# Pooling the keys with a halving addition and accumulating products instead of a reduction

## The chip, the cores and the metric

One core of a Trainium2 chip runs the whole program. Its engines are TensorE (PE in the profile; its loads of the stationary operand are PEld), VectorE (DVE), ScalarE (ACT), GpSimd (POOL) and SyncE (SP), which issues most of the DMAs. Each engine works through its own instructions in the order in which they were written and waits on semaphores for the others. The metric is the device time of one execution in microseconds; lower is better.

## The reference

Three layers one after the other, all in float32:

```python
# attention, B, H, S, D = 4, 8, 576, 64; keys and values are pooled by 8
k_p = k.reshape(B, H, S // 8, 8, D).mean(axis=3)        # 72 pooled keys per head
v_p = v.reshape(B, H, S // 8, 8, D).mean(axis=3)
scores = np.matmul(q, k_p.transpose(0, 1, 3, 2)) / np.sqrt(D)
attn = softmax(scores);  x = np.matmul(attn, v_p)       # -> x: 2304 tokens x 512

# a mixture of 8 experts with balanced shares P (8 rounds of row and column scaling)
for e in range(8):
    out += P[:, e:e+1] * (np.maximum(x @ w1[e], 0) @ w2[e])

# one more layer: softplus(x @ w_in) @ w_out, 512 -> 2048 -> 512
```

The change touches only the pooling of the keys and values, that is `k_p` and `v_p`.

## The kernel before, in words

**Attention in steps.** The attention is cut into 32 steps, m = 0 to 31. A step takes one pair of heads and half of the 576 queries of one batch (288, in three tiles of 96). The first ten steps, m < AHEAD = 10, run at the front of the kernel with nothing else beside them but the preparation of the first expert weights (`sums_w1(0)` after step 4, `prep_w1(0)` after step 6). The other 22 are laid between the products of the experts, which keep TensorE busy for the rest of the run.

**One step** (`attn_step`, L391): TensorE turns the queries of the next step, channels first (`pq`, L288; ScalarE copies them to `qT`), and multiplies those of this step with the block-diagonal pooled keys `kbd` (`s`, L311). VectorE takes the maximum of each row (`mx`, L317) and subtracts it (`ex`, L318), ScalarE takes the exponential. One step later VectorE sums and inverts (`divide`, L325 to L327), GpSimd multiplies (L328). Another step later TensorE turns the result (`pa`, L339), ScalarE copies it to `aT`, and TensorE multiplies it with the pooled values `vp` (`px`, L349, `mix`); ScalarE copies `px` to the input of the experts.

**Pooling** (`pool_kv`, L265). A pair of heads of one batch has one tile of keys `kt` and one of values `vt`, each 72 partitions x 2 heads x 8 positions x 64 channels. There are 16 pairs, i = 0 to 15. The keys are summed over the 8 positions by one VectorE reduction (`kp`, L269). The values of the first four pairs are summed by three halving additions on GpSimd (L271 to L273), the others by a VectorE reduction (L275). `keys_first` (L293) then turns `kp` on TensorE into a bank `pk` with a transpose (L297), and VectorE scales the two halves of it into `kbd` (L299).

**Order.** Everything is written out by hand. `pool_at` says at the end of which step a pair is pooled, and `turn_at` in which step its keys are turned: one step later. Pairs 0 and 1 are pooled ahead of step 0, pair 2 in step 0, pair 3 in step 1, pairs 4 to 7 in steps 3, 5, 7 and 9, and pair 8 in step 11. Within a step the order is: turn the queries, scores and maximum, the gate of finished tokens, turn the older softmax, turn the keys that were pooled in the step before, exponential, divide, mix, and at the end pool the next pair. Loads of further keys and values are issued behind the pooling of a pair (L278).

After step 9 the tokens of the first group are split into differences and remainders (`ta`, L437; `xhi`, L467; `xlo`, L471), and the products of the experts begin (`p`, L530).

Of the kernel before, what the change touches and what calls it, by code (L numbers as in the profile page):

```python
# [9 lines left out]
F32 = mybir.dt.float32  # L10
# [3 lines left out]
ALU = mybir.AluOpType  # L14
AX = mybir.AxisListType
# [4 lines left out]
def attention_moe_softplus_kernel(  # L20
# [12 lines left out]
    nc = tc.nc  # L33
    B, H, S, D = q.shape
# [4 lines left out]
    POOL = 8  # L39
    SP = S // POOL  # L40
    HP = H // 2
# [37 lines left out]
    def bank(name, kind="y", dt=F32):  # L79
        kind = kind if kind in banks else ""  # L80
        return banks[kind].tile([P, 512], dt, tag=f"bank{kind}", name=name)
# [7 lines left out]
    ident = cpool.tile([P, P], F32, name="ident")  # L89
# [74 lines left out]
    def pool_add(o, a, b):  # L164
        nc.gpsimd.tensor_tensor(o, a, b, op=ALU.add)
# [53 lines left out]
    at_p = actx.enter_context(tc.tile_pool(name="at", bufs=2))  # L219
# [8 lines left out]
    AHEAD = 10  # L228
# [13 lines left out]
    def load_kv(pool):  # L242
        i = next_kv[0]
        if i >= B * HP:
            return
        next_kv[0] += 1
        b, h0 = i // HP, i % HP * 2
        kt = pool.tile([SP, 2, POOL, D], F32, tag="k", name="kt")
        vt = pool.tile([SP, 2, POOL, D], F32, tag="v", name="vt")
        nc.sync.dma_start(kt, k[b, h0:h0 + 2].rearrange("h (p t) d -> p h t d", t=POOL))  # L250
        nc.sync.dma_start(vt, v[b, h0:h0 + 2].rearrange("h (p t) d -> p h t d", t=POOL))
        kv_t[i] = kt, vt, pool
# [11 lines left out]

    def pool_kv(i):  # L265
        kt, vt, pool = kv_t.pop(i)
        kp = at_p.tile([SP, 2, D], F32, tag="kp", name="kp", bufs=1)
        vp = at_p.tile([SP, 2, D], F32, tag="vp", name="vp", bufs=NK + 1)
        nc.vector.tensor_reduce(kp, kt.rearrange("p h t d -> p h d t"), axis=AX.X, op=ALU.add)  # L269
        if i < HP:  # L270
            pool_add(vt[:, :, 0:4, :], vt[:, :, 0:4, :], vt[:, :, 4:8, :])  # L271
            pool_add(vt[:, :, 0:2, :], vt[:, :, 0:2, :], vt[:, :, 2:4, :])
            pool_add(vp, vt[:, :, 0, :], vt[:, :, 1, :])  # L273
        else:
            nc.vector.tensor_reduce(vp, vt.rearrange("p h t d -> p h d t"), axis=AX.X, op=ALU.add)  # L275
        pooled[i] = kp, vp

        if pool is ld_p or next_kv[0] < 2 * HP:  # L278
            load_kv(pool)

    def channels_first(m):

        qt = q_l.pop(m)
        pq = bank("pq")
        qT = at_p.tile([P, W], F32, tag="qT", name="qT")
        for j in range(JH):
            src = qt[:, j].rearrange("p h d -> p (h d)")
            nc.tensor.transpose(pq[:, j * QP:(j + 1) * QP], src, ident[:QP, :QP])  # L288
        nc.scalar.copy(qT, pq[:, :W])
        q_t[m] = qT  # L290
        load_q(m + NQ)

    def keys_first(i):  # L293

        kp = pooled[i][0]
        pk = bank("pk")
        nc.tensor.transpose(pk[:, :SP], kp.rearrange("p h d -> p (h d)"), ident[:SP, :SP])  # L297
        for h in range(2):
            nc.vector.tensor_scalar_mul(  # L299
                kbd[i % NK][h * D:(h + 1) * D, h * SP:(h + 1) * SP],  # L300
                pk[h * D:(h + 1) * D, :SP],
                1.0 / POOL / math.sqrt(D),
            )
# [29 lines left out]
    def turn_attn():  # L333
        m, ex = to_turn.pop(0)
        aT = at_p.tile([SP, 2, W], F32, tag="aT", name="aT")
        for h in range(2):
            pa = bank("pa")
            for j in range(JH):
                nc.tensor.transpose(pa[:SP, j * QP:(j + 1) * QP], ex[:, 2 * j + h, :], ident[:QP, :QP])  # L339
            nc.scalar.copy(aT[:, h, :], pa[:SP, :W])  # L340
        to_mix.append((m, aT))
# [38 lines left out]


    pool_at = {}
    for i in range(2, B * HP):
        b, hp = divmod(i, HP)
        pool_at.setdefault(hp - 2 if b == 0 else 2 * HP * b - 5 + 2 * hp, []).append(i)
    turn_at = {}
    for m, l in pool_at.items():
        turn_at.setdefault(m + 1, []).extend(l)
    turn_at.setdefault(0, []).append(1)

    def attn_step(m, early):  # L391


        last = STEPS
        if m + 1 < last:
            channels_first(m + 1)
        if m < last:
            exp, divide = softmax(m)
        while to_gate:
            gate()  # L400
        while to_turn:
            turn_attn()
        for i in turn_at.get(m, ()):
            keys_first(i)
        if m < last:
            exp()
            to_divide.append(divide)
        while len(to_divide) > (1 if early else 0):
            to_divide.pop(0)()
        while len(to_mix) > (0 if early or m >= last else 1):  # L410
            mix()
        for i in pool_at.get(m, ()):
            pool_kv(i)

    for i, pool in enumerate((ld_e, ld_e, ld_p, ld_p)):
        load_kv(pool)
# [6 lines left out]
    load_w(1, 0)  # L423
    load_w(2, 0)
    pool_kv(0)
    channels_first(0)
    keys_first(0)
    pool_kv(1)
    nc.gpsimd.memset(ones, 1.0)

# [602 lines left out]
```

## Time and profile before

| | |
|---|---|
| time, median of 3 runs | 2063.92 us (2063.12 to 2064.44) |
| profiled execution: its span, the one time that its page gives | 2065.1 us |
| TensorE busy | 2021.1 us, 98% of the span |
| VectorE busy | 1446.1 us, 70% |
| GpSimd busy | 1233.9 us, 60% |
| ScalarE busy | 837.6 us, 41% |

The profile records one execution. Its page gives the busy time of each engine and the chain of work that ended last, followed back from the end: at each step to what released it. A timeline lists the instructions by their start; the column after the start is how long they took, and the bracket at the end is the idle time of the engine just before, with what ended it. A stretch of time can be cut into windows, with busy time, granted clock of TensorE (1.00 is the full 2.4 GHz, 0.50 the lower level of 1.2 GHz) and the share of the DMA engines. A matrix product or a transpose can show up as several instructions, and matmul ends are modelled, since they are pipelined.

### The profile page before, as it was taken

What the parts mean: (1) busy time and instruction counts of PE and PEld (TensorE: products, weight loads), DVE (VectorE), ACT (ScalarE), POOL (GpSimd) and SP (SyncE); (2) the same over time, 40 slices, a digit from 0 to 9 for tenths busy, and PEclk for the clock granted to TensorE, in tenths of its full rate; (3) what the DMA queues carried; (4) which work ended last, traced back from release to release, by engine and by line L of the source; (5) the groups of instructions that cost most, each with busy time, mean ns of one, the idle gap of its engine ahead of it and who ended that gap; (6) DMA issues with size and microseconds to landing.
All of it is one profiled execution on the core that took longest, in us unless ns stands there. A gap on an engine that the chain in (4) does not pass through costs nothing.

```text
span 2065.1 us, 27617 instructions
## 1 busy us (share of the span) xinstructions
PE 2021.1 (98%) x10285; PEld 1746.1 (85%) x10285; DVE 1446.1 (70%) x2477; ACT 837.6 (41%) x1583; POOL 1233.9 (60%) x993
## 2 busy tenths in 40 slices
PE   7899999999999999999999999999999999999998
PEld 5677888888888888888888888888888888888887
DVE  7787587875666767777776776777777666767756
ACT  4555545454322433222243222222222356565554
POOL 4666689886556555556565555655555554544555
PEclk9799999999999999999999999999999999999999
DMA  6353233444223222232242222322222111121132
GB/s 183 89 141 108 86 94 103 142 150 144 67 92 126 76 92 86 82 92 78 91 154 72 87 82 77 92 73 86 92 82 82 62 53 50 62 87 52 62 118 72
DMA packets 133762, 192.00 MB, mean 93 GB/s; under 512 B 26924, under 2 KB 82940, under 8 KB 133628
## 3 DMA queue, kind: packets, MB, share of 16 engines
q1 hardware_dynamic: 129596, 183.82, 28.5%
q10 hardware_dynamic: 4032, 6.42, 0.8%
q8 instruction: 80, 1.31, 0.3%
q14 instruction: 54, 0.44, 0.1%
HBM read 166.94 MB, written 23.27 MB: 92 GB/s over the span
## 4 chain that ended last, share of the span: by engine, by line
PE 88%; DVE 6%; ACT 3%; POOL 2%; issue 1%; DMA 1%; SPq 0%; ACTq 0%; POOLq 0%; DVEq 0%
PE py L530 44%; PE p L530 32%; PE ph L530 9%; POOL w1lo L168 1%; DVE kp L269 1%; PE s L311 1%; ACT w1hi L199 1%; DVE vp L275 1%; PE px L349 1%; PE pa L339 0%; POOL w2lo L168 0%; PE pt L692 0%; ACT xhi L467 0%; DVE mx L317 0%; DVE s L325 0%
## 5 line engine op out<-in xcount | busy, mean ns | idle before, releaser
L530 PE MATMUL py<-w2hi,hhi 128*128 128x512 f32 x1440 | 567.9, 394 | 5.0 <-DVE g L686 2.7
L530 PE MATMUL py<-w2hi,hlo 128*128 128x512 f32 x1440 | 562.7, 391 | 0.8 <-POOL hlo L573 0.8
L530 PE MATMUL py<-w2lo,hhi 128*128 128x512 f32 x1440 | 562.5, 391 | 0.0
L168 POOL TENSOR_TENSOR w1lo<-w1raw,w1hi 128x512 fp32r<-128x512 f32 (+1 forms) x216 | 252.2, 1186 | 458.2 <-ACT w1hi L199 357.8
L530 PE MATMUL p<-xhi,w1hi 128*128 128x448 f32 (+1 forms) x1344 | 459.9, 342 | 9.8 <-DVE p L610 3.6
L530 PE MATMUL p<-xlo,w1hi 128*128 128x448 f32 (+1 forms) x1344 | 457.7, 341 | 3.4 <-DVE xlo L471 3.3
L530 PE MATMUL p<-xhi,w1lo 128*128 128x448 f32 (+1 forms) x1344 | 457.3, 340 | 3.7 <-POOL w1lo L168 3.7
L686 DVE SCALAR_TENSOR_TENSOR g<-py,prob,g 128x512 f32<-128x512 f32 x482 | 360.4, 748 | 99.2 <-PE py L530 87.8
L545 ACT ACTIVATE hhi<-p 128x448 fp32r<-128x448 f32 (+1 forms) x384 | 180.9, 495 | 414.1 <-PE p L530 380.1
L530 PEld LDWEIGHTS py<-w2hi,hhi 128*128 128x128 f32 x1440 | 271.2, 188 | 65.9 <-DVE g L686 4.6
L530 PEld LDWEIGHTS py<-w2hi,hlo 128*128 128x128 f32 x1440 | 271.0, 188 | 60.9 <-POOL hlo L573 1.7
L168 POOL TENSOR_TENSOR w2lo<-w2raw,w2hi 128x1024 fp32r<-128x1024 f32 x120 | 289.0, 2408 | 51.5 <-ACT w2hi L212 46.3
L530 PEld LDWEIGHTS py<-w2lo,hhi 128*128 128x128 f32 x1440 | 271.3, 188 | 49.9
L530 PEld LDWEIGHTS p<-xhi,w1hi 128*128 128x128 f32 x1344 | 256.5, 191 | 38.4 <-DVE p L610 4.7
L530 PEld LDWEIGHTS p<-xlo,w1hi 128*128 128x128 f32 x1344 | 256.6, 191 | 22.6 <-DVE xlo L471 3.9
L530 PEld LDWEIGHTS p<-xhi,w1lo 128*128 128x128 f32 x1344 | 256.9, 191 | 17.8 <-POOL w1lo L168 4.9
L612 ACT COPY za<-p 128x448 f32<-128x448 f32 (+1 forms) x96 | 46.0, 479 | 477.0 <-PE p L530 472.8
L546 DVE SCALAR_TENSOR_TENSOR hlo<-p,hhi 128x448 fp32r<-128x448 f32 (+1 forms) x384 | 210.3, 549 | 32.9 <-ACT hhi L545 32.4
L168 POOL TENSOR_TENSOR w1lo<-sums,w1hi 128x1024 fp32r<-128x1024 f32 x96 | 231.4, 2410 | 0.0
L610 DVE TENSOR_TENSOR za<-p,za 128x448 f32<-128x448 f32 (+1 forms) x96 | 53.4, 556 | 166.9 <-PE p L530 166.8
L780 POOL TENSOR_TENSOR dt<-dt,dr 128x512 f32<-128x512 f32 x32 | 41.5, 1295 | 150.5 <-DVE dr L779 150.5
L573 POOL TENSOR_TENSOR hlo<-ln,hhi 128x448 fp32r<-128x448 f32 (+1 forms) x80 | 97.3, 1218 | 51.8 <-ACT hhi L572 51.5
(123 smaller groups left out, 2707.6 us busy)
## 6 DMA issues: line engine op xcount, KB each, us to landing
w1raw<-in_moe_w_dram SPq DMA_DIRECT2D x96, 512.0 KB
w2raw<-in_moe_w_dram SPq DMA_DIRECT2D x96, 512.0 KB
w1raw<-v SPq DMA_DIRECT2D x24, 512.0 KB
w2raw<-v SPq DMA_DIRECT2D x24, 512.0 KB
f<-in_moe_w_in_dram SPq DMA_DIRECT2D x16, 512.0 KB
v<-dt SPq DMA_DIRECT2D x32, 256.0 KB
f<-in_moe_w_out_dram SPq DMA_DIRECT2D x16, 512.0 KB
xlod<-xl ACTq DMA_DIRECT2D x28, 224.0 KB
```

Source lines behind the costliest of these rows:

```text
L168: nc.gpsimd.tensor_tensor(o, a, b, op=ALU.subtract)
L199: nc.scalar.copy(at(hi), src)
L269: nc.vector.tensor_reduce(kp, kt.rearrange("p h t d -> p h d t"), axis=AX.X, op=ALU.add)
L275: nc.vector.tensor_reduce(vp, vt.rearrange("p h t d -> p h d t"), axis=AX.X, op=ALU.add)
L530: nc.tensor.matmul(ps, lhs[a], rhs[b], start=first and i == 0, stop=last and i == 2, skip_group_check=goes_on,)
L545: nc.scalar.activation(hh, src, AF.Relu)
L546: nc.vector.scalar_tensor_tensor(hl, src, 0.0, hh.bitcast(F32), op0=ALU.max, op1=ALU.subtract)
L573: nc.gpsimd.tensor_tensor(hl, l, hh.bitcast(F32), op=ALU.subtract)
L610: add = lambda o, x, y: nc.vector.tensor_tensor(o, x, y, op=ALU.add)
L612: nc.scalar.copy(a, pa)
L686: nc.vector.scalar_tensor_tensor(a, py, prob[:, t, e:e + 1], a, op0=ALU.mult, op1=ALU.add)
L780: nc.gpsimd.tensor_tensor(t, t, r.bitcast(F32), op=ALU.add)
```

## The change

For the pairs that are pooled in steps 0 to 9 and ahead of them (i = 0 to 7), the reduction and the transpose of the keys go. In their place VectorE adds the second four positions of `kt` onto the first four, in place, and TensorE multiplies what is left, position by position and head by head, with the identity, and accumulates: eight products of 72 x 64 with 72 x 72 that leave the pooled keys, already channels first, in `pk`. The scaling into `kbd` stays. The keys of such a pair are now turned in the step in which it is pooled and not in the next, and the pooling stands ahead of the exponential, the division and the mix, not at the step's end. The values of pairs 4 to 7 move from a VectorE reduction to the three GpSimd additions. Pairs 8 to 15 are pooled and turned as before.

```diff
--- before.py
+++ after.py
@@ -264,16 +264,21 @@
 
     def pool_kv(i):
         kt, vt, pool = kv_t.pop(i)
-        kp = at_p.tile([SP, 2, D], F32, tag="kp", name="kp", bufs=1)
         vp = at_p.tile([SP, 2, D], F32, tag="vp", name="vp", bufs=NK + 1)
-        nc.vector.tensor_reduce(kp, kt.rearrange("p h t d -> p h d t"), axis=AX.X, op=ALU.add)
-        if i < HP:
+        early = pooled_at[i] < AHEAD
+        kp = None
+        if not early:
+            kp = at_p.tile([SP, 2, D], F32, tag="kp", name="kp", bufs=1)
+            nc.vector.tensor_reduce(kp, kt.rearrange("p h t d -> p h d t"), axis=AX.X, op=ALU.add)
+        if early:
             pool_add(vt[:, :, 0:4, :], vt[:, :, 0:4, :], vt[:, :, 4:8, :])
             pool_add(vt[:, :, 0:2, :], vt[:, :, 0:2, :], vt[:, :, 2:4, :])
             pool_add(vp, vt[:, :, 0, :], vt[:, :, 1, :])
         else:
             nc.vector.tensor_reduce(vp, vt.rearrange("p h t d -> p h d t"), axis=AX.X, op=ALU.add)
         pooled[i] = kp, vp
+        if early:
+            keys_first(i, kt)
 
         if pool is ld_p or next_kv[0] < 2 * HP:
             load_kv(pool)
@@ -290,11 +295,21 @@
         q_t[m] = qT
         load_q(m + NQ)
 
-    def keys_first(i):
+    def keys_first(i, kt=None):
 
         kp = pooled[i][0]
         pk = bank("pk")
-        nc.tensor.transpose(pk[:, :SP], kp.rearrange("p h d -> p (h d)"), ident[:SP, :SP])
+        if kt is None:
+            nc.tensor.transpose(pk[:, :SP], kp.rearrange("p h d -> p (h d)"), ident[:SP, :SP])
+        else:
+            half = POOL // 2
+            nc.vector.tensor_tensor(kt[:, :, 0:half, :], kt[:, :, 0:half, :], kt[:, :, half:POOL, :], op=ALU.add)
+            for t in range(half):
+                for h in range(2):
+                    nc.tensor.matmul(
+                        pk[h * D:(h + 1) * D, :SP], kt[:, h, t, :], ident[:SP, :SP],
+                        start=t == 0, stop=t == half - 1,
+                    )
         for h in range(2):
             nc.vector.tensor_scalar_mul(
                 kbd[i % NK][h * D:(h + 1) * D, h * SP:(h + 1) * SP],
@@ -380,13 +395,15 @@
 
 
     pool_at = {}
+    pooled_at = {0: -1, 1: -1}
     for i in range(2, B * HP):
         b, hp = divmod(i, HP)
-        pool_at.setdefault(hp - 2 if b == 0 else 2 * HP * b - 5 + 2 * hp, []).append(i)
+        pooled_at[i] = hp - 2 if b == 0 else 2 * HP * b - 5 + 2 * hp
+        pool_at.setdefault(pooled_at[i], []).append(i)
     turn_at = {}
     for m, l in pool_at.items():
-        turn_at.setdefault(m + 1, []).extend(l)
-    turn_at.setdefault(0, []).append(1)
+        if m >= AHEAD:
+            turn_at.setdefault(m + 1, []).extend(l)
 
     def attn_step(m, early):
 
@@ -402,6 +419,9 @@
             turn_attn()
         for i in turn_at.get(m, ()):
             keys_first(i)
+        if m < AHEAD:
+            for i in pool_at.get(m, ()):
+                pool_kv(i)
         if m < last:
             exp()
             to_divide.append(divide)
@@ -409,8 +429,9 @@
             to_divide.pop(0)()
         while len(to_mix) > (0 if early or m >= last else 1):
             mix()
-        for i in pool_at.get(m, ()):
-            pool_kv(i)
+        if m >= AHEAD:
+            for i in pool_at.get(m, ()):
+                pool_kv(i)
 
     for i, pool in enumerate((ld_e, ld_e, ld_p, ld_p)):
         load_kv(pool)
@@ -424,7 +445,6 @@
     load_w(2, 0)
     pool_kv(0)
     channels_first(0)
-    keys_first(0)
     pool_kv(1)
     nc.gpsimd.memset(ones, 1.0)
```

The order of TensorE's instructions from the program's start to the scores of step 1, before (`pq` turned queries, `s` scores, `pk` pooled keys; the number at `kbd` is the buffer, one per pair of heads):

```order
L288 MATMUL pq<-ident,qt 128x96 x3
L297 MATMUL pk<-ident,kp 128x72
L288 MATMUL pq<-ident,qt 128x96 x3
L311 MATMUL s<-kbd_126,qT 96x144 x3
L297 MATMUL pk<-ident,kp 128x72
L288 MATMUL pq<-ident,qt 128x96 x3
L311 MATMUL s<-kbd_127,qT 96x144 x3
```

And the same stretch after the change:

```order
L309 MATMUL pk<-ident,kt 64x72 x8
L293 MATMUL pq<-ident,qt 128x96 x3
L309 MATMUL pk<-ident,kt 64x72 x8
L293 MATMUL pq<-ident,qt 128x96 x3
L326 MATMUL s<-kbd_126,qT 96x144 x3
L309 MATMUL pk<-ident,kt 64x72 x8
L293 MATMUL pq<-ident,qt 128x96 x3
L326 MATMUL s<-kbd_127,qT 96x144 x3
```

The keys of pair 1 now stand ahead of the scores of step 0, and those of pair 2 ahead of the scores of step 1; before, each stood behind them.

VectorE's instructions in step 3, to the maximum of step 4, before (`s` in the rows of L325 and L326 is the row sum; `vp` pooled values):

```order
L317 TENSOR_REDUCE mx<-s 96x6
L318 TENSOR_TENSOR ex<-s,mx 96x432
L325 TENSOR_REDUCE s<-ex 96x6
L326 TENSOR_SCALAR s<-s 96x6
L327 RECIPROCAL sm<-s 96x6
L269 TENSOR_REDUCE kp<-kt 72x128
L275 TENSOR_REDUCE vp<-vt 72x128
L317 TENSOR_REDUCE mx<-s 96x6
```

And after:

```order
L332 TENSOR_REDUCE mx<-s 96x6
L333 TENSOR_TENSOR ex<-s,mx 96x432
L306 TENSOR_TENSOR kt<-kt 72x2x256
L314 TENSOR_SCALAR kbd_130<-pk 64x72 x2
L340 TENSOR_REDUCE s<-ex 96x6
L341 TENSOR_SCALAR s<-s 96x6
L342 RECIPROCAL sm<-s 96x6
L332 TENSOR_REDUCE mx<-s 96x6
```

The two reductions behind the division are gone. Ahead of it stand the halving addition and the two scalings, which read what TensorE makes of that addition.

GpSimd's instructions from the preparation of the first weights (`w1lo`, after step 6) on, before (`ex` is the multiplication of L328):

```order
L168 TENSOR_TENSOR w1lo<-w1raw,w1hi 128x512
L168 TENSOR_TENSOR w1lo<-w1raw,w1hi 128x256
L168 TENSOR_TENSOR w1lo<-sums,w1hi 128x1024
L328 TENSOR_TENSOR ex<-ex,sm 96x432 x3
L437 TENSOR_TENSOR tb<-g_92 128x512
```

And after:

```order
L168 TENSOR_TENSOR w1lo<-w1raw,w1hi 128x512
L168 TENSOR_TENSOR w1lo<-w1raw,w1hi 128x256
L168 TENSOR_TENSOR w1lo<-sums,w1hi 128x1024
L165 TENSOR_TENSOR vt<-vt 72x2x256
L165 TENSOR_TENSOR vt<-vt 72x2x128
L165 TENSOR_TENSOR vp<-vt 72x128
L343 TENSOR_TENSOR ex<-ex,sm 96x432 x2
L165 TENSOR_TENSOR vt<-vt 72x2x256
L165 TENSOR_TENSOR vt<-vt 72x2x128
L165 TENSOR_TENSOR vp<-vt 72x128
L343 TENSOR_TENSOR ex<-ex,sm 96x432
```

The additions for the values of pair 6 stand between the weights and the multiplication of step 7, and those of pair 7 ahead of the multiplication of step 9.

## Rows read from the trace of the kernel before

**Rows 1.** Chain of waits, 0 to 110 us, its shares by line.

```profile
by line: PE p L530 16.3%; DVE kp L269 8.4%; PE py L530 7.7%; PE s L311 6.5%; POOL w1lo L168 5.4%; PE px L349 5.3%; DVE vp L275 4.9%; PE pa L339 4.5%; DMA kt<-in_k_dram 4.1%; issue 3.7%; DVE mx L317 3.6%; DVE s L325 3.0%; DVE ex L318 2.8%; P
```

**Rows 2.** Windows: length, busy PE, PEld, DVE, ACT, POOL, then clock, DMA share, GB/s.

```profile
20.00:28.00 8.00, 8.00 (x36) 6.27 (x35) 5.90 (x10) 3.27 (x8) 1.81 (x2) 1.00 0.87 233
28.00:40.00 12.00, 8.73 (x86) 5.60 (x84) 11.28 (x24) 7.25 (x22) 5.21 (x7) 1.00 0.46 112
42.00:50.00 8.00, 7.47 (x32) 5.15 (x30) 5.61 (x9) 3.47 (x10) 4.29 (x4) 0.50 0.65 178
```

**Rows 3.** Groups by shape, 0 to 60 us: busy us, mean ns | idle before.

```profile
L269 DVE TENSOR_REDUCE kp<-kt 72x128 f32<-72x1024 f32 x8 | 15.1, 1892 | 4.8 <-DMA kt<-in_k_dram 4.8
...
L275 DVE TENSOR_REDUCE vp<-vt 72x128 f32<-72x1024 f32 x4 | 7.6, 1900 | 0.0
...
L299 DVE TENSOR_SCALAR kbd<-pk 64x72 f32<-64x72 f32 x14 | 3.2, 226 | 1.5 <-PE pk L297 1.4
...
L471 DVE TENSOR_TENSOR xlo<-tb,xhi 128x512 fp32r<-128x512 f32 x1 | 1.3, 1346 | 0.3 <-ACT xhi L467 0.3
...
L471 DVE TENSOR_TENSOR xlo<-ta,xhi 128x512 fp32r<-128x512 f32 x1 | 0.7, 692 | 0.0
```

**Rows 4.** Timeline of the opening, steps 0 to 2: start us, length us.

```profile
8.16 1.90 DVE L269 TENSOR_REDUCE kp<-kt 72x128 f32<-72x1024 f32 x1 [0.39 <-DMA kt<-in_k_dram]
...
10.09 0.60 DVE L317 TENSOR_REDUCE mx<-s 96x6 f32<-96x432 f32 x1
...
13.10 2.06 POOL L165 TENSOR_TENSOR vt<-vt 72x512 f32<-72x512 f32 x2 [0.92 <-DMA vt<-in_v_dram]
...
13.68 0.60 DVE L317 TENSOR_REDUCE mx<-s 96x6 f32<-96x432 f32 x1
...
15.24 0.45 POOL L165 TENSOR_TENSOR vp<-vt 72x128 f32<-72x128 f32 x1
...
17.36 1.17 PE L339 MATMUL pa<-ident,ex 96*72 96x96 f32 x6 [0.18 <-POOL ex L328]
```

**Rows 5.** Timeline of step 3 and the start of step 4.

```profile
20.17 0.74 PE L288 MATMUL pq<-ident,qt 96*128 96x96 f32 x3
...
20.70 1.65 PE L311 MATMUL s<-kbd,qT 128*96 128x144 f32 x6
...
22.39 0.60 DVE L317 TENSOR_REDUCE mx<-s 96x6 f32<-96x432 f32 x1 [1.86 <-PE s L311]
...
23.31 1.70 PE L349 MATMUL px<-aT,vp 72*64 72x288 f32 x4
...
23.62 0.60 DVE L325 TENSOR_REDUCE s<-ex 96x6 f32<-96x432 f32 x1
...
24.57 1.88 DVE L269 TENSOR_REDUCE kp<-kt 72x128 f32<-72x1024 f32 x1
...
24.95 0.74 PE L288 MATMUL pq<-ident,qt 96*128 96x96 f32 x3
```

**Rows 6.** Timeline, steps 5 to 9 and the first products of the experts.

```profile
29.20 0.47 PE L288 MATMUL pq<-ident,qt 96*128 96x96 f32 x3
...
34.15 0.90 PE L311 MATMUL s<-kbd,qT 128*96 128x144 f32 x6
...
34.98 0.69 PE L371 MATMUL pg<-g,wg 128*8 128x72 f32 x32
...
38.01 0.47 PE L288 MATMUL pq<-ident,qt 96*128 96x96 f32 x3
...
42.14 2.38 POOL L168 TENSOR_TENSOR w1lo<-sums,w1hi 128x1024 fp32r<-128x1024 f32 x1
...
44.46 0.92 POOL L328 TENSOR_TENSOR ex<-ex,sm 96x432 f32<-96x432 f32 x1
...
48.25 0.74 PE L288 MATMUL pq<-ident,qt 96*128 96x96 f32 x3
...
57.57 0.58 PE L530 MATMUL p<-xlo,w1hi 128*128 128x256 f32 x1 [3.27 <-DVE xlo L471]
```

## The prediction

> **What bounds the kernel now.** I read the chain of waits first, for the stretch up to 110 us, since the change touches nothing but the first ten attention steps and the first products behind them. There the reader sees the reductions of the keys with 8.4% and those of the values with 4.9% of 110 us, 14.6 us together [rows 1]: VectorE's pooling is on the path that sets the end. Everything behind is the experts' products, which follow from whenever the front is done, so a microsecond gained or lost in the front is one in the total. Then the windows: from 28 to 40 us VectorE is busy for 11.28 of 12 us and TensorE for 8.73, so VectorE bounds there; from 20 to 28 us TensorE is busy for all 8 us and VectorE for 5.90, and from 42 to 50 us TensorE for 7.47 us and VectorE for 5.61 [rows 2]. So the bound changes hands, and TensorE's clock decides it: from 42 to 50 us the granted clock is 0.50, which is 1.2 GHz, and from 28 to 40 us it is 1.00, 2.4 GHz. For 20 to 28 us the column says 1.00, but the six score instructions take 1.65 us there and 0.90 us later [rows 5, 6], so I take the opening to run at the lower level. Last the timeline, step by step, from one start of a turn of queries to the next: steps 3 to 5 take 9.03 us (20.17 to 29.20), 5 to 7 take 8.81 and 7 to 9 take 10.24 [rows 5, 6].
>
> **What the change removes.** Eight reductions of keys of 1.89 us and four of values of 1.90 us [rows 3], 22.7 us of VectorE. It adds eight halving additions of 72 x 512; the row of the same shape and kind over 128 partitions, a remainder, is 0.69 us [rows 3], so 5.5 us. VectorE's two scalings (0.226 us each, 0.45 us together) stay.
>
> **What it adds on TensorE.** Eight products per pair instead of one transpose. The trace has no such group, so I bound it. From below: the gate's 32 instructions of the same moving width, 72, take 0.69 us at the full level [rows 6]; a program's float32 product shows as two instructions, so 16 instructions at that rate are 0.35 us, or 0.63 us at the lower level, by the ratio 1.65/0.90 of the scores. From above: six score instructions with twice the columns (144), one behind the other, take 1.65 us at the lower level [rows 5]; sixteen of half the width, none beside another, are 2.2 us. The gate writes to four groups of columns at once, the new products to two, so I take twice the gate's time: 0.69 us at the full level, 1.27 us at the lower. That is the nearest row; a gain below zero is excluded, as 16 instructions replace one.
>
> **What it moves, and what then waits.** This decides. Before, a reduction ran one step ahead, while TensorE did the scores, and its transpose stood behind them. Now VectorE's halving stands behind the subtraction of its own step, the products wait for it on TensorE, the two scalings wait for the products on VectorE, and behind them wait the division of the last step, GpSimd's multiplication and so TensorE's next turn. On TensorE the next step's queries and scores are queued behind the products, though they don't need those keys yet.
>
> Opening. The keys of pair 1 land at about 8.1 us, as VectorE's wait shows [rows 4]. Then: halving 0.69, products 1.27, queries and scores 2.18 (20.17 to 20.70 + 1.65) [rows 5]: the maximum of step 0 starts at 12.3 us, not at 10.09 [rows 4]. From one maximum to the next it was 3.59 us (10.09 to 13.68 [rows 4]), set by VectorE; now it is the loop maximum and subtraction 1.23 (22.39 to 23.62 [rows 5]), halving 0.69, products 1.27, queries and scores 2.18, 5.4 us. The maximum of step 1 is at 17.7 us; then 1.23 + 0.69 + 1.27, scalings 0.45, division 0.95 (23.62 to 24.57), multiplication 0.92 [rows 3, 5, 6] lead to the first turn of a softmax at 23.2 us, where it was at 17.36 [rows 4]. **+5.9 us.** Nothing absorbs it: VectorE's reductions wait 4.8 us in all for keys to land [rows 3], for the first two pairs alone.
>
> Steps 3 to 5, at the lower level: the products start after 2.18 + 1.23 + 0.69 = 4.1 us, end at 5.4, the mix and the way to the next step are 1.64 us (23.31 to 24.95 [rows 5]): 7.0. The even step is TensorE's 4.78 us (20.17 to 24.95). 11.8 against 9.03, **+2.8 us.**
>
> Steps 5 to 7: before, full level came at about 28 us, after TensorE had worked with hardly a gap from 17.36 us on [rows 2, 4]. I expect the same about 11 us into the new steps 3 and 4, so full level here. TensorE's terms times 0.55: 1.2 + 1.23 + 0.69 + 0.69 = 3.8 to the end of the products; 0.45 + 0.95 + 0.92 until the next softmax can be turned, 6.1; then turn, copy and mix about 2 us: 8.1 us. The three additions of the values, 2.06 + 0.45 = 2.51 us [rows 4], stand ahead of the multiplication on GpSimd, which has the sums of the first weights in that step too; I add 1.0 for them. 9.1 against 8.81, **+0.3 us** (at the lower level 11.8, +3.0).
>
> Steps 7 to 9: GpSimd's `w1lo` ends at 44.52, 6.5 us behind the start of step 7, and the multiplication that waits for it starts then; from there to step 9 it is 3.79 us (44.46 to 48.25) [rows 6]. Now the value additions of pair 6 stand between: 6.5 + 2.51 + 3.79 = 12.8 against 10.24, **+2.5 us.** This is where moving the values costs: before, VectorE's reduction lay beside `w1lo`.
>
> Step 9: two reductions no longer stand ahead of the differences. Before, the first remainder's product starts 9.32 us into the step (48.25 to 57.57 [rows 6]). Now 2.18 + 1.23 + 0.69 + 1.27 + 0.45 + 0.95 = 6.8, then a difference and a remainder of 0.69 and 0.4 for the rounding between: 8.6, **-0.7 us.** The gain of 3.8 us of reductions is spent on the wait for the products.
>
> Both engines at once: a remainder over 128 x 512 took 0.692 us with VectorE nearly alone and 1.346 us beside GpSimd's own [rows 3]. The halvings of pairs 2, 5 and 6 meet GpSimd's additions: pair 2's values land at 13.10 us and take 2.51 us [rows 4], across its halving at 13.5. Each is 0.65 us longer; I count half of 2.0, **+1.0 us.** The Trainium skill (GPSIMD Engine Reference, section 1, Specifications) says that GpSimd shares its SBUF interfaces with VectorE, in contention where a VectorE instruction has two SBUF inputs; the reduction that goes has one, the addition that comes has two. The two rows agree; without that rule the sum would be 1.0 us less.
>
> **Sum.** 5.9 + 2.8 + 0.3 + 2.5 - 0.7 + 1.0 = +11.8 us. The profiled span is 2065.1 us and the median of the runs 2063.9, so they differ by 1.2 us; I add to the median: **2075.7 us**. SP's loads keep their order but for one store behind two loads, so they add nothing; a keys' tile is freed by products instead of a reduction, later by less than the queue is ahead.
>
> **Rivals.**
> - Faster, by VectorE's relief: the five key reductions (9.3 us) and three of values (5.4 us) on the path [rows 1] give way to five halvings, 3.4 us: 14.6 - 3.4 = 11.2 us less, 2052.7. For it: VectorE is busy for 94% of 28 to 40 us [rows 2]. Against it: this needs the products and scalings to be done before VectorE would be at the division, and the order puts nothing between the halving and the scalings that wait for them. It decides from the point where the products take under 0.4 us and the front runs at the full level from the start. Chance 0.10.
> - Full level early, since TensorE now does products where it did transposes: then 0.69 and 1.2 stand for 1.27 and 2.18. The first maximum is at 10.7, the loop 3.8, the first turn at 19.5, +2.1; steps 3 to 5 take 8.1, -0.9; the rest +0.3, +2.5, -0.7, +1.0: +4.3 us, 2068.2. For it: the same kind of work reached 1.00 by 28 us; against it: 42 to 50 us, busy for 93% at 0.50 [rows 2]. Chance 0.15.
> - Lower level throughout the front, since TensorE waits more: +3.0 for +0.3, and the whole 2.0 for both engines: +15.5 us, 2079.4. Chance 0.13.
>
> **How the numbers follow.** The forecast has 0.62. The products' ends, 0.63 and 2.2 us at the lower level, move six groups on the path by -0.64 and +0.93 us each: +8 to +17 us. With the rivals on its side the range is 2066 to 2083; below it lie the first rival and a little of the second. A change within 0.2%, 4.1 us, can't be told from none here. Faster 0.10; within 0.2% half of the second rival and a small rest of the forecast, 0.13; slower 0.77.
>
> **What would show it.** Right: maxima of steps 0, 1 and 2 more than 5 us apart; VectorE idle between halving and scaling, released by `pk`; the first turn of a softmax near 23 us; GpSimd with three value additions between `w1lo` and a multiplication that TensorE waits for; the experts' first products some 12 us later and all behind them unchanged. Wrong: products of a key group well under a microsecond at the lower level, scores that are not held up by them, a granted clock of 1.00 from the first steps on, or the experts starting no later than at 58 us.

## The result, and the profile after

The change makes the kernel slower: 2076.39 us median of 4 runs (2073.38 to 2078.33) against 2064.18 us (2063.12 to 2068.86), a ratio of 1.0055 with an interval of 1.0039 to 1.0070; the medians are 12.2 us apart. The profiled execution was the slowest of the four, 2078.33 us; its span is 2076.5 us, 11.4 us more than the span before. VectorE is busy for 1434.1 us, 12.0 us less than before, and GpSimd for 1244.1 us, 10.2 us more: the work moved as intended, and the end came later all the same.

The opening, in the timeline of the changed kernel (start us, length us; the bracket is the idle time before and what ended it):

```profile
12.40 0.60 DVE L332 TENSOR_REDUCE mx<-s 96x6 f32<-96x432 f32 x1 [1.56 <-PE s L326]
...
13.56 1.33 DVE L306 TENSOR_TENSOR kt<-kt 72x512 f32<-72x512 f32 x1
...
14.95 1.23 PE L309 MATMUL pk<-ident,kt 72*64 72x72 f32 x16 [2.58 <-DVE kt L306]
...
16.30 0.47 DVE L314 TENSOR_SCALAR kbd<-pk 64x72 f32<-64x72 f32 x2 [1.40 <-PE pk L309]
...
18.33 0.60 DVE L332 TENSOR_REDUCE mx<-s 96x6 f32<-96x432 f32 x1 [1.56 <-PE s L326]
...
23.60 0.60 DVE L332 TENSOR_REDUCE mx<-s 96x6 f32<-96x432 f32 x1 [0.61 <-PE s L326]
...
24.10 1.18 PE L354 MATMUL pa<-ident,ex 96*72 96x96 f32 x6 [0.53 <-POOL ex L343]
```

The maxima of steps 0, 1 and 2 start at 12.40, 18.33 and 23.60 us, 5.93 and 5.27 us apart, where the first two started at 10.09 and 13.68 [rows 4]. The reader can walk round one loop: maximum at 12.40, halving from 13.56 to 14.89, products from 14.95, for which TensorE had waited 2.58 us, scalings at 16.30 behind a wait of 1.40, and the next maximum at 18.33, which waited for scores that stood on TensorE behind those products. The first softmax is turned at 24.10 us, not at 17.36 [rows 4].

The groups by shape and the sums of waits over the first 75 us, the stretch that answers to [rows 3] (busy us, mean ns | idle before; then engine and instruction, what released it: sum us, count, longest):

```profile
L309 PE MATMUL pk<-ident,kt 72*64 72x72 f32 x128 | 8.3, 295 | 17.6 <-DVE kt L306 11.6 <-issue 6.0
...
L306 DVE TENSOR_TENSOR kt<-kt 72x512 f32<-72x512 f32 x8 | 7.2, 904 | 5.4 <-DMA kt<-in_k_dram 5.4
```

```profile
DVE mx L332 <- PE s L326: 20.0, 10, 5.7
...
PE pk L309 <- DVE kt L306: 11.6, 4, 5.2
...
DVE kbd L314 <- PE pk L309: 9.6, 8, 1.5
```

TensorE's products wait 11.6 us in all for the halving (5.2 of them at the start) and 6.0 more for which the profile shows no releaser ("issue"). These 6.0 us are waits for the halving too: in the timeline each of the four ends about 0.1 us behind the end of a halving, the one before 41.51 us, for instance, behind the halving that ended at 41.41. VectorE's scalings wait 9.6 us for the products, VectorE's maxima 20.0 us for the scores (4.1 us in the first 60 us before the change), the halvings themselves 5.4 us for keys to land. A ring of three waits took the place of the reductions.

Later steps, in the same timeline:

```profile
26.91 0.74 PE L293 MATMUL pq<-ident,qt 96*128 96x96 f32 x3
...
37.35 0.47 PE L293 MATMUL pq<-ident,qt 96*128 96x96 f32 x3
...
39.82 1.59 DVE L306 TENSOR_TENSOR kt<-kt 72x512 f32<-72x512 f32 x1
...
40.14 0.72 POOL L168 TENSOR_TENSOR sums<-sums,w1raw 128x256 f32<-128x256 f32 x1
...
41.51 0.72 PE L309 MATMUL pk<-ident,kt 72*64 72x72 f32 x16 [1.96 <-issue]
...
43.24 1.65 PE L326 MATMUL s<-kbd,qT 128*96 128x144 f32 x6
...
48.31 0.47 PE L293 MATMUL pq<-ident,qt 96*128 96x96 f32 x3
...
52.02 2.34 POOL L168 TENSOR_TENSOR w1lo<-sums,w1hi 128x1024 fp32r<-128x1024 f32 x1
...
54.33 2.05 POOL L165 TENSOR_TENSOR vt<-vt 72x512 f32<-72x512 f32 x2
...
56.87 1.77 POOL L343 TENSOR_TENSOR ex<-ex,sm 96x432 f32<-96x432 f32 x2
...
57.83 1.18 PE L354 MATMUL pa<-ident,ex 96*72 96x96 f32 x6 [2.98 <-POOL ex L343]
...
60.64 0.74 PE L293 MATMUL pq<-ident,qt 96*128 96x96 f32 x3
...
67.58 2.64 DVE L491 TENSOR_TENSOR xlo<-g,xhi 128x512 fp32r<-128x512 f32 x1
...
68.41 1.26 POOL L457 TENSOR_TENSOR tb<-g 128x512 f32<-128x512 f32 x1
...
70.27 0.58 PE L550 MATMUL p<-xlo,w1hi 128*128 128x256 f32 x1 [2.35 <-DVE xlo L491]
```

Step 3 starts at 26.91, step 5 at 37.35, step 7 at 48.31, step 9 at 60.64 and the first remainder's product at 70.27 us; before they started at 20.17, 29.20, 38.01, 48.25 and 57.57 [rows 5, 6]. The delay so grows from 6.74 to 8.15, 10.30, 12.39 and 12.70 us. It falls to 11.1 us by the first product of the second layer of the first expert (89.19 before, 100.27 after), and the spans differ by 11.4. Three stalls stand out: the halving of pair 5 took 1.59 us beside GpSimd's sums and TensorE waited 1.96 us ahead of 41.51; GpSimd's three value additions lie between `w1lo` and the multiplication at 56.87, and TensorE waited 2.98 us for it; the first remainder took 2.64 us beside the multiplication and `tb` on GpSimd.

TensorE's windows (columns as in [rows 2]):

```profile
35.00:42.00 7.00, 4.44 (x42) 3.20 (x43) 4.80 (x8) 3.22 (x8) 4.02 (x6) 1.00 0.18 42
42.00:46.00 4.00, 4.00 (x54) 2.94 (x50) 2.31 (x7) 0.81 (x2) 3.26 (x4) 0.57 0.18 41
46.00:52.00 6.00, 3.65 (x38) 2.71 (x40) 2.92 (x7) 5.58 (x16) 3.25 (x3) 1.00 0.01 3
52.00:62.00 10.00, 6.96 (x40) 4.78 (x36) 3.42 (x10) 3.55 (x10) 8.89 (x10) 0.54 0.51 143
```

The clock is at the full level (2.4 GHz) from 35 us: the scores took 1.65 us at 33.79 and 0.90 us at 37.65. It is 0.57 in the mean from 42 to 46 us, so mostly at the lower level (1.2 GHz), right behind a stretch in which TensorE was busy for 4.44 of 7 us, and is at 0.54 again from 52 us on.

### The profile page after: what moved, and what is told of

The parts are those of the page before. It is cut to its first block, busy times and chain, and to the rows that moved or that the text cites. A ratio compares the mean times of both kernels' runs of the same rounds, so it can differ in the third digit from the quotient of the medians.

```text
span 2076.5 us, 27866 instructions
## 1 busy us (share of the span) xinstructions
PE 2024.8 (98%) x10405; PEld 1750.6 (84%) x10405; DVE 1434.1 (69%) x2473; ACT 837.7 (40%) x1583; POOL 1244.1 (60%) x1005
## 3 DMA queue, kind: packets, MB, share of 16 engines
q8 instruction: 81, 1.33, 0.3%
## 4 chain that ended last, share of the span: by engine, by line
PE 82%; DVE 2%; ACT 2%; POOL 1%; issue 0%; DMA 0%; ACTq 0%; POOLq 0%; SPq 0%; DVEq 0%
PE py L550 42%; PE p L550 30%; PE ph L550 9%; ACT w1hi L199 1%; PE pt L712 0%; ACT xhi L487 0%; POOL w1lo L168 0%; ACT hhi L565 0%; DMA f<-in_moe_w_in_dram 0%; POOL w2lo L168 0%; DVE g L859 0%; DVE g L706 0%; DVE c L581 0%; ACT ln L582 0%; DVE hlo L566 0%
```

## The experiments

The change does two things: other operations, and another place for them. The first two runs take one of each.

**The new operations in the old order (e1).** The halving goes back to the end of its step, the products to the next step behind the scores, as the transposes stood. The main lines of the edit:

```diff
         if early:
-            keys_first(i, kt)
+            half = POOL // 2
+            nc.vector.tensor_tensor(kt[:, :, 0:half, :], kt[:, :, 0:half, :], kt[:, :, half:POOL, :], op=ALU.add)
+            halved[i] = kt, pool
+            return
...
-        if m >= AHEAD:
-            turn_at.setdefault(m + 1, []).extend(l)
+        turn_at.setdefault(m + 1, []).extend(l)
```

> The new operations in the old order: the halving at the end of a step, the eight products and the scalings in the next step, behind the scores and the turned softmax; pairs 4 to 7 keep their value additions on GpSimd, also at the end of a step. Theory (the order costs, since scores queue behind the products and the division behind the scalings): the opening is back, first turn of a softmax at 16 to 18 us instead of 24.1, steps 3 to 9 no longer than before, 2059 to 2066 us. Rival (the operations themselves cost: products of 1.2 us, contention of halvings and additions): 2070 us or more.

Measured: 2069.60 us against 2064.93, ratio 1.0019 [1.0010, 1.0028]. The opening is back: maxima 3.62 us apart, first turn of a softmax at 18.83 us, and the first remainder's product at 55.64 us, 1.9 us earlier than before the change. But the queries of step 11 came 10.6 us after that product, not 3.2 as before. The timeline there:

```profile
58.32 6.65 DVE L495 TENSOR_TENSOR xlo<-ta,xhi 128x512 fp32r<-128x512 f32 x1
...
58.67 1.26 POOL L461 TENSOR_TENSOR tb<-g 128x512 f32<-128x512 f32 x1
...
63.70 0.71 POOL L168 TENSOR_TENSOR sums<-sums,w1raw 128x256 f32<-128x256 f32 x1
...
64.49 1.06 POOL L168 TENSOR_TENSOR sums<-w1raw,sums 128x256 f32<-128x256 f32 x1
...
66.26 0.68 PE L296 MATMUL pq<-ident,qt 96*128 96x96 f32 x3
```

One remainder on VectorE took 6.65 us (0.69 in [rows 3]), while GpSimd went from `tb` to the sums of the next weights; the queries of step 11 stand behind its product. So neither expectation held whole: the order accounts for most of the loss, and the new operations bring a loss of their own at another place.

**The new order with the old operations (e2).** Reductions and transposes, placed as the change places its halvings and products.

```diff
-        if not early:
+        if True:
             kp = at_p.tile([SP, 2, D], F32, tag="kp", name="kp", bufs=1)
             nc.vector.tensor_reduce(kp, kt.rearrange("p h t d -> p h d t"), axis=AX.X, op=ALU.add)
-        if early:
+        if i < HP:
...
         if early:
-            keys_first(i, kt)
+            keys_first(i)
+        if i >= HP:
+            nc.vector.tensor_reduce(vp, vt.rearrange("p h t d -> p h d t"), axis=AX.X, op=ALU.add)
```

> The old operations in the new order: reductions of keys and transposes, but in the step in which the pair is pooled and ahead of the division, the value reductions of pairs 4 to 7 on VectorE behind the scalings. Theory (order): as slow as the change or slower, since 1.89 us of reduction and 0.33 us of transpose stand in the loop instead of 0.69 and 1.23 us: about 5.7 us from one maximum to the next in the opening, first turn of a softmax at 24 to 26 us, 2078 to 2086 us. Rival (operations): near before, 2064 to 2068 us.

Measured: 2083.26 us against 2064.93, ratio 1.0081 [1.0068, 1.0095]. Its timeline:

```profile
12.80 0.60 DVE L332 TENSOR_REDUCE mx<-s 96x6 f32<-96x432 f32 x1 [1.38 <-PE s L326]
...
15.91 0.38 PE L303 MATMUL pk<-ident,kp 72*128 72x72 f32 x1 [3.15 <-DVE kp L272]
...
18.25 0.60 DVE L332 TENSOR_REDUCE mx<-s 96x6 f32<-96x432 f32 x1 [1.38 <-PE s L326]
...
24.43 1.18 PE L354 MATMUL pa<-ident,ex 96*72 96x96 f32 x6 [0.71 <-POOL ex L343]
```

The maxima are 5.45 us apart with a single transpose of 0.38 us for the products: the loop is as long as the change's without any of its operations. The order alone costs more than the change does. From pair 4 on it has two parts here: the reduction of the keys and also that of the values now stand ahead of the division, so not all of the 18 us is the queue behind the keys.

**The values back on VectorE (e3).** The change, but the values of pairs 4 to 7 by a reduction behind the scalings.

```diff
-        if early:
+        if i < HP:
...
             keys_first(i, kt)
+        if i >= HP:
+            nc.vector.tensor_reduce(vp, vt.rearrange("p h t d -> p h d t"), axis=AX.X, op=ALU.add)
```

> The change, but the values of pairs 4 to 7 are summed by a VectorE reduction again, behind the scalings. Theory (value additions ahead of GpSimd's multiplication cost 2.5 us in steps 7 to 9): these two steps shrink from 12.3 us to about 10.5, while the 1.9 us of reduction ahead of the division makes steps 3 to 5 and 5 to 7 up to 1.5 us longer each; 2073 to 2079 us in all. Rival (steps 7 to 9 are set by the products and the clock): they stay at 12 us or more.

Measured: 2083.35 us against 2064.93, ratio 1.0084 [1.0069, 1.0098], a miss: slower than the change. Steps 7 to 9 took 14.8 us, not less than the change's 12.3. The timeline of step 7:

```profile
55.61 2.33 POOL L168 TENSOR_TENSOR w1lo<-sums,w1hi 128x1024 fp32r<-128x1024 f32 x1
...
55.80 2.70 DVE L306 TENSOR_TENSOR kt<-kt 72x512 f32<-72x512 f32 x1
...
60.37 1.91 DVE L281 TENSOR_REDUCE vp<-vt 72x128 f32<-72x1024 f32 x1
```

With the additions gone from GpSimd the step met `w1lo` elsewhere: the halving of pair 6, 0.68 us in the change, took 2.70 us beside it, and behind the scalings the reduction held the division for 1.91 us more. In the trace of the change the value additions hold the multiplication for 2.5 us; what they cost in the end this run does not isolate, since their removal in this order costs more. It shows something else beside e2, though. The two kernels differ in one thing, the operations on the keys: reduction and transpose in e2, halving and eight products here. Their times can't be told apart (1.0081 and 1.0084). So in this order the new operations on the keys bring nothing that can be measured, and the 7 us, by the medians, by which the change is faster than both come with the move of the values to GpSimd.

**The values alone (e4).** The kernel before, with the values of pairs 4 to 7 on GpSimd at the end of the step.

```diff
-        if i < HP:
+        if i < 2 * HP:
```

> The kernel before with one part of the change alone: the values of pairs 4 to 7 by three additions on GpSimd, at the end of a step as there. Theory (the additions hurt only where a multiplication stands behind them that TensorE waits for): VectorE's relief of 1.9 us shows in steps 5 to 7 and at step 9, 2059 to 2064 us. Rival (the additions on GpSimd cost wherever they stand): 2066 us or more.

Measured: 2063.83 us against 2064.93, ratio 0.9993 [0.9984, 1.0002]: within the expected range, at its upper end, and not told apart from before. The rival is out. In the trace the first remainder's product came at 52.96 us, 4.6 us earlier than before, and the queries of step 11 at 57.79, only 3.0 us earlier, so part of the gain goes at the handover to the experts; a gain of 3.0 us in all lies within the interval. Not all of the 4.6 us is VectorE's relief: 0.5 us stand ahead of the first instruction that differs, since in this execution step 4's turn of queries was already at the full level (0.47 us, 0.74 before).

**The old order in the opening alone (e5).** The change, with pairs 0 to 3 in the order of e1; the edit is against e1.

```diff
             halved[i] = kt, pool
+            if i >= HP:
+                keys_first(i)
             return
...
-        turn_at.setdefault(m + 1, []).extend(l)
+        if m < 2 or m >= AHEAD:
+            turn_at.setdefault(m + 1, []).extend(l)
...
+        if 2 <= m < AHEAD:
+            for i in pool_at.get(m, ()):
+                pool_kv(i)
```

> The change, but pairs 0 to 3 in the old order (halving at the end of a step, products one step later); pairs 4 to 7 as the change has them. Theory (the opening's loss is the order): the first softmax is turned at about 18.8 us, as in the run with the old order throughout, instead of 24.1, and the rest is as with the change, 2069 to 2074 us. Rival (what the opening gains is lost again later, since GpSimd or the clock sets the pace): 2075 us or more.

Measured: 2070.88 us against 2063.93, ratio 1.0031 [1.0020, 1.0042]. Its timeline:

```profile
18.35 1.18 PE L363 MATMUL pa<-ident,ex 96*72 96x96 f32 x6 [0.46 <-POOL ex L352]
...
21.57 0.74 PE L298 MATMUL pq<-ident,qt 96*128 96x96 f32 x3
```

Step 3 starts at 21.57 us, 5.3 us earlier than in the change, so 5.3 of the opening's 6.7 us are the order. By the medians the whole is 5.5 us shorter than the change, inside the theory's range. That it arrives one to one is not shown: in this trace the first remainder's product comes at 66.75 us, only 3.5 us earlier than in the change, since steps 3 to 7 took longer here (23.2 us, 21.4 in the change), with scores of 1.65 us up to step 6. The rival's point, that the clock can take back what the opening gains, holds for a part.

**No halving at all (e7).** The change with sixteen products over the full keys in place of the addition and eight.

```diff
-            half = POOL // 2
-            nc.vector.tensor_tensor(kt[:, :, 0:half, :], kt[:, :, 0:half, :], kt[:, :, half:POOL, :], op=ALU.add)
+            half = POOL
```

> The change without the halving: sixteen accumulating products of a position and head, straight from the loaded keys, in the change's order; VectorE only scales. Theory (what costs is that scores are queued behind products that wait for VectorE): the products take about 2.2 us at the lower level but wait for nothing, so a step of the opening is 4.4 us instead of 5.3 to 5.9, the first softmax is turned at about 22 us, 2069 to 2075 us. Rival (the products' own time is the price, and it doubles): first turn at 26 us or later, 2079 us or more.

Measured: 2069.91 us against 2063.93, ratio 1.0026 [1.0015, 1.0037]; its median is 6.5 us below the change's and 6.0 above before. Its timeline:

```profile
12.96 2.19 PE L308 MATMUL pk<-ident,kt 72*64 72x72 f32 x32
...
13.07 0.60 DVE L331 TENSOR_REDUCE mx<-s 96x6 f32<-96x432 f32 x1 [1.56 <-PE s L325]
...
17.30 0.60 DVE L331 TENSOR_REDUCE mx<-s 96x6 f32<-96x432 f32 x1 [1.56 <-PE s L325]
...
22.03 1.17 PE L353 MATMUL pa<-ident,ex 96*72 96x96 f32 x6 [0.53 <-POOL ex L342]
```

The products take 2.19 us instead of 1.23, and the maxima are 4.23 us apart instead of 5.3 to 5.9, since TensorE no longer waits for VectorE. So the main price of the change is not the time of the products but the wait for the halving, with everything queued behind it. The products are not free: here they are 2.19 of the 4.23 us of a loop that took 3.59 before, and the kernel stays slower than before.

**What the new operations cost at the handover (e6, e10).** Both start from e1. e6 takes GpSimd's last three additions away (the values of pair 7 by a reduction in step 10; one load moves along with it); e10 gives VectorE the parts of the first split that GpSimd had. The edits, e6's first:

```diff
+        if i == 2 * HP - 1:
+            late_values.append((vp, vt))
...
+        if m == AHEAD:
+            vp, vt = late_values.pop()
+            nc.vector.tensor_reduce(vp, vt.rearrange("p h t d -> p h d t"), axis=AX.X, op=ALU.add)
```

```diff
-    first_sums = t_sums(x_of(0), t0_of, on_pool=(2,))
-    first_splits = splits("moe", x_of(0), t0_of, on_pool=(2, 4))
+    first_sums = t_sums(x_of(0), t0_of)
+    first_splits = splits("moe", x_of(0), t0_of)
```

> The new operations in the old order, as in the first experiment, but the values of pair 7 are summed by a VectorE reduction in step 10, behind the first products of the experts, not on GpSimd at the end of step 9. Theory (what was left of the loss there is the collision of these additions and of what GpSimd does behind them with VectorE's two-input remainders, one of which took 6.65 us): the stretch from the first remainder's product to the queries of step 11 is 3 to 4 us again instead of 10.6, 2060 to 2066 us. Rival (the products of the key groups cost it): 2068 us or more.

> The new operations in the old order, as in the first experiment, but the one difference and two remainders of the splits that ran on GpSimd are on VectorE too. Theory (the 10.6 us from the first remainder's product to the queries of step 11 come from VectorE's two-input instructions standing still while GpSimd works through its own without a gap): with three instructions of 0.7 us more VectorE is still done sooner, the stretch is 6 to 8 us, no remainder takes over 4 us, 2064 to 2068 us. Rival (the stretch is set by the value additions themselves or by ScalarE): 10 us or more, 2069 us or more.

e6: 2063.12 us against 2063.93, ratio 0.9995 [0.9986, 1.0004]; from the first remainder's product to the queries of step 11 it is 3.2 us again, and e1's loss is gone:

```profile
57.82 0.58 PE L561 MATMUL p<-xlo,w1hi 128*128 128x256 f32 x1 [2.27 <-DVE xlo L502]
...
61.04 0.68 PE L298 MATMUL pq<-ident,qt 96*128 96x96 f32 x3
```

Nor is there a gain: eleven of VectorE's reductions are gone against eight halvings, a twelfth comes later, and the first remainder's product comes at 57.82 us, where it came at 57.57 before. One halving took 3.23 us beside `w1lo` and a remainder 2.62 us beside `tb`. A position in one trace is good to about 1 us here: e1 and e6 have the same instructions up to the end of step 9, but step 4's turn of queries took 0.47 us in e1 and 0.74 us, the lower level, in e6.

e10: 2067.34 us against 2064.25, ratio 1.0017 [1.0008, 1.0026]; the same stretch is 8.1 us (56.65 to 64.73). Its longest stall:

```profile
59.44 2.87 DVE L461 TENSOR_TENSOR tb<-g,ta 128x512 f32<-128x512 f32 x1
...
61.05 0.71 POOL L168 TENSOR_TENSOR sums<-sums,w1raw 128x256 f32<-128x256 f32 x1
```

Without GpSimd's part of the split no instruction of VectorE took more than 3 us there, but VectorE had the work of both, and the sums still held one difference for 2.87 us. The stretch came near its theory (6 to 8 us), and the time is in the expected range, but the ratios of e1 and e10 can't be told apart. The loss of e1 is so tied to the two engines' work at the handover: it goes when GpSimd has less there (e6), and hardly when VectorE has more (e10).

**Towards a faster kernel (e8, e9).** Both keep the reductions of the keys and the order of before. e8 takes the values of pairs 4 to 6 to GpSimd and reduces those of pair 7 in step 10; e9 reduces them in step 9, where they were. e9's edit is shown; e8 does the same for these pairs and has, beside that, e6's later reduction of pair 7:

```diff
-        if i < HP:
+        if i < 2 * HP - 1:
```

> The kernel before with reductions and transposes in the old order, but the values of pairs 4 to 6 by additions on GpSimd at the end of a step, and those of pair 7 by a VectorE reduction in step 10. Theory (VectorE's relief counts from step 4 on, and the splits meet no additions): the first remainder's product at about 52 us instead of 57.6 and the queries of step 11 at 56 instead of 60.8, 2057 to 2062 us, faster than both kernels. Rival (the moved reduction holds up the first expert, or the clock gives it back): 2063 us or more.

> The kernel before with the values of pairs 4, 5 and 6 by additions on GpSimd at the end of a step, and those of pair 7 by VectorE's reduction in step 9 as before, so that GpSimd does its difference for the splits beside one-input reductions. Theory (VectorE's relief in steps 5 to 8 is kept, about 2 us, and the splits run as before): queries of step 10 at about 46 us instead of 48.25, 3 to 4 us from the first remainder's product to the queries of step 11, 2060 to 2063 us. Rival (the gain is given back behind the front whatever the splits do): 2063.5 us or more.

e8: 2063.25 us against 2063.93, ratio 0.9996 [0.9987, 1.0005], a miss: the first remainder's product came at 53.73 us and the queries of step 11 at 59.94, not at 56. Its timeline, and that of e9:

```profile
50.87 4.18 POOL L334 TENSOR_TENSOR ex<-ex,sm 96x432 f32<-96x432 f32 x1 [3.66 <-DVE sm L333]
...
54.32 3.73 DVE L447 TENSOR_TENSOR tb<-g,ta 128x512 f32<-128x512 f32 x1
...
56.24 1.25 POOL L481 TENSOR_TENSOR xlo<-ta,xhi 128x512 fp32r<-128x512 f32 x1
```

```profile
51.26 1.18 POOL L328 TENSOR_TENSOR ex<-ex,sm 96x432 f32<-96x432 f32 x1 [3.65 <-DVE sm L327]
...
52.40 1.27 POOL L437 TENSOR_TENSOR tb<-g 128x512 f32<-128x512 f32 x1
...
52.80 1.88 DVE L275 TENSOR_REDUCE vp<-vt 72x128 f32<-72x1024 f32 x1
...
54.60 0.67 DVE L437 TENSOR_TENSOR ta<-g 128x512 f32<-128x512 f32 x1
```

In e8 GpSimd's multiplication shows 4.18 us and ends once VectorE's run of two-input instructions breaks; then one of VectorE's differences takes 3.73 us beside GpSimd. In e9 the multiplication took 1.18 us, and `tb` lies beside VectorE's reductions, before VectorE's two-input instructions begin. e9: 2061.06 us against 2064.25, ratio 0.9991 [0.9982, 0.9999]. That is in the expected range, and its queries of step 10 (46.61 us) and the stretch to those of step 11 (3.2 us) came as expected. It is the lowest ratio of the ten runs, with an interval that only just leaves out no change; but among ten intervals one can do that by chance, and it overlaps those of e4, e6 and e8. That any version is faster than the kernel before is not shown.

## Why the prediction was right, point by point

The forecast was 2075.7 us, 11.8 above the kernel before, and the medians came out 12.2 apart. The mechanism is the one that happened: the products wait for the halving, the scalings for the products, and division, multiplication and the next turn stand behind them. By its own terms:

| stretch | predicted, us | measured, us |
|---|---|---|
| opening, to step 3 | +5.9 | +6.7 |
| steps 3 to 5 | +2.8 | +1.4 |
| steps 5 to 7 | +0.3 | +2.2 |
| steps 7 to 9 | +2.5 | +2.1 |
| step 9 to the first remainder's product | -0.7 | +0.3 |
| both engines at once | +1.0 | within the rows above |
| sum to the first remainder's product | +11.8 | +12.7 |
| spans | +11.8 | +11.4 |

- **Products.** A group of sixteen instructions was put at 1.27 us at the lower level and 0.69 at the full one; it took 1.23 and 0.72. Twice the gate's time was the right reading of [rows 6], and it excludes the first rival, which needed under 0.4 us.
- **Opening.** The first turn was forecast at 23.2 us and came at 24.10; the first maximum at 12.3 and came at 12.40; the loop at 5.4 and was 5.93 and 5.27. The 0.65 us by which pair 2's halving outlasted 0.68 is the term that the prediction kept apart. (Its own terms, 23.2 less 17.36, give +5.8 and not +5.9.) e2, e5 and e7 show that the loss is made by the order, as the prediction had it.
- **Steps 3 to 5, mis-sized.** The products started 4.2 us into step 3, as forecast (4.1), but the mix behind them took 1.20 us, where one took 1.70 at the lower level before, and the step 6.35 us, forecast 7.0. Step 4 took 4.09 us, forecast 4.78: full level came at about 35 us, inside the step, and not at its end.
- **Steps 5 to 7, mis-sized.** The full level was taken for granted here. The halving of pair 5 was held for 1.59 us, TensorE stood for 1.96 us before its products, and the clock was 0.57 from 42 to 46 us, so the scores at 43.24 took 1.65 us again. Of the 2.2 us, 0.7 fell in step 5 and 1.45 in step 6, where the turn of queries, the scores and the gate took 1.48 us longer than at the full level before. The rival "lower level throughout", with +3.0 here, came near in size for these two steps.
- **Steps 7 to 9.** As forecast: the additions stood between `w1lo`, which ended at 54.36, and the multiplication at 56.87, and TensorE waited 2.98 us. What the prediction took this for is not borne out: it calls the move of the values a cost, but without the move the kernel is 7 us slower in this order (e3), and in the old order the move makes no difference that can be measured (e4). The additions show as a wait here, but in this order the reductions that they replace cost more.
- **Step 9.** The gain of 0.7 us did not come. The remainder was put at 0.69 us and took 2.64, held by GpSimd's multiplication and `tb`. The rest of the step was 0.9 us shorter than forecast, in the main since the products took 0.72 us here and not 1.27.
- **Both engines at once.** The halvings of pairs 0 to 7 took 0.69, 0.91, 1.33, 0.68, 0.68, 1.59, 0.68 and 0.68 us by the timeline, 1.8 us over eight times 0.68; the prediction set 2.0 and counted half. Of the pairs that it named, 2 and 5 were lengthened and 6 was not; the remainder, which it did not name, was. Pair 6's did run beside `w1lo`, but there the two first instructions of `w1lo` took 2.40 us, not 1.96 as before: GpSimd paid. The price of 0.65 us was read off one row as if it were fixed; that remainder, from 59.84 to 61.19 us before the change, also ended 0.56 us behind an instruction of GpSimd (59.36 to 60.63), so it too had stood for what was left of it.
- **After the front** 1.3 us of the delay are given back between the first remainder's product and the spans, 1.6 us already by the first product of the second layer. The prediction had all behind the front unchanged. The two traces show where 1.5 us of that went: 24 products of the first expert took 4.47 us before (65.45 to 69.92), most of them 0.41 us each, with a clock of 0.62 in the mean, and 3.01 us after (78.08 to 81.09), 0.28 us each at 1.00. Why the clock stood otherwise there, no run tells.

That the sum came so close is partly luck, since terms were off in opposite directions: 1.4 too much in steps 3 to 5, 0.4 in steps 7 to 9 and 1.0 for both engines at once, against 0.8 too little in the opening, 1.9 in steps 5 to 7 and 1.0 in step 9.

## What to carry to other kernels

Moving work off a busy engine pays only if no engine then waits in order for the result with independent work behind it: the same reductions, only placed in the step that needs them and ahead of the division, cost more than the whole change, and keeping the producer one step ahead took most of the loss away. Where the time of a moved piece is in question, look at the ring of waits before the length of the piece: twice the products without the halving was faster than the change, though still slower than before. And count what the relief is worth at the end: with the old order and no additions at the handover, eleven reductions fewer gave no gain that could be measured (e6). Lastly, before a VectorE operation with one input is replaced by one with two, look at what GpSimd does beside it.

## What the runs showed of the hardware

A VectorE instruction with two inputs in SBUF that meets GpSimd's work is not slowed down in proportion; it stands, and then finishes. The rows above have the numbers: the halving at 39.82 us of the changed kernel ended at 41.41, 0.55 us behind the end of GpSimd's sum at 40.86; its remainder ended at 70.22, 0.55 us behind `tb`; in e1 the remainder of 6.65 us ended at 64.97, 0.56 us behind the sum that ended at 64.41; in e3 the halving of 2.70 us 0.56 us behind `w1lo`; in e8 the difference of 3.73 us 0.56 us behind GpSimd's remainder; in e10 that of 2.87 us 0.55 us behind a sum. In the first 95 us of the twelve traces 57 of VectorE's halvings, differences and remainders took over 0.86 us; every one of them ended between 0.54 and 0.56 us behind the end of a GpSimd instruction. So the price is not the instruction's own time but what is left of GpSimd's run, up to 6.0 us over the 0.69 us that it takes alone. The Trainium skill (SBUF — State Buffer, section "Summary: rules for kernel authors") says that where a VectorE instruction has two SBUF inputs while GpSimd's reads SBUF, the second one to issue fully blocks until the first finishes. The runs agree that it blocks, but not that the wait always ends with the first: it can last over several GpSimd instructions; by the timeline, e1's remainder stood through six whole ones, from `tb` to the third sum. At some ends between two of them VectorE came in (in e1 between the multiplication that ended at 55.04 us and the additions of the values), at others not; what decides that, these runs do not show. Where VectorE came in, it was the next GpSimd instruction that took longer: the additions of the values took 2.51 us beside e5's halving at 36.24 us, which kept its 0.71 us, and 2.06 us elsewhere.

The other way round it is less clear. GpSimd's multiplication of 0.91 us showed 4.17 us in e4 and 4.18 us in e8, and ended 0.76 to 0.77 us behind a gap in VectorE's run of two-input instructions. But in both it began under a reduction with one input, as it did in e9, where it took 1.18 us. The spans of GpSimd are rough, and this stays open.
